# Queries in a four-block ring, and re-layout reads for one block at a time

## The chip, the cores and the metric

The kernel runs on one core of one Trainium2 chip. The metric is the device time of the whole program in microseconds (us), median of several runs. Before the change it is 1012.76 us (three runs: 1012.76, 1017.84, 1010.63).

## The reference

A pre-norm transformer layer in float32 on 2048 tokens of width 640: attention with 32 heads of 20, a causal sliding window of 256 keys, then a gated feed-forward of width 1536.

```
h  = x + softmax(mask(q k^T / sqrt(20))) v @ wo     with q,k,v = layernorm(x) @ wqkv
h2 = h + (gelu(layernorm(h) @ w_gate) * (layernorm(h) @ w_up)) @ w_down
mask: 0 <= i - j < 256
```

The kernel keeps float32 accuracy with float16 operands by splitting each operand into a high and a low half and adding three products.

## The kernel before

**Tiles.** The 2048 tokens are 16 blocks of 128 (index j) and 8 chunks of two blocks (index c). Queries and keys are projected a chunk at a time (`qk`, dense work on TensorE), values a block at a time (`vproj`). Scores and maxima work on a block and a pair of heads: 16 pairs for each block, and each block looks at three key blocks, its own and the two before it.

**Queries and keys on the way.** The projection leaves features on partitions in an order that the scores cannot use. So `qk_out` splits the result into halves (tile `qks`) and writes them to a DRAM tensor `qk` (a DMA issued by ACT), and `stack` reads that back in the layout that the scores need: tile `qT` for queries, the ring `kT` of six blocks (RK = 6) for keys. Each `stack` issues six DMAs, each of 20 partitions by 16 head pairs, on SP. There are two stacks for a chunk, so 12 reads of 160 KB for each chunk. The queries of a chunk have one tile `qT` from a pool with two buffers, so chunk c goes into the buffer that chunk c - 2 used. Before that the two buffers hold the raw query weights.

**Maxima, scores, values.** `maxima` multiplies queries (60 rows) by keys into the PSUM buffer `ra` or `rb`, and DVE takes the row maximum (`junk<-ra,band`, result in `mxs`). When all 32 heads of a block have one, the maximum is turned and written into rows 60 and 61 of `qT` (`qT<-mT`, a DMA issued by ACT), and `scores` computes the keys-by-queries product with the maximum already taken off (62 rows), ACT takes the exponential (`pt`), POOL masks it, and `value_lane` multiplies by the values into `pv`. The TensorE groups of maxima and scores come in pairs, one in `ra` and one in `rb`; between the pairs stand values and dense work.

**What sets the order.** Nothing is ordered by hand. A planner (the loop at the end of `block_kernel`) runs a clock for every engine and issues the next instruction of that lane which its clock says is ready, so a change in when one tile is free re-orders all engines. Each engine then executes its own list strictly in order on the chip. A `stack` begins when the planner's conditions hold: for chunks 0 and 1 when the split query weights are ready, later when block 2c - 3 has all its values (`B[2 * c - 3].scored`), which frees `qT` and the two key slots. From chunk 2 on there is also a pacing condition (`PACE`) ahead of each read, so other transfers come between. SP issues the input rows (`xt<-in_x_dram`, which the layer norm on DVE reads: `lstx<-xt`), the transposes of the normed rows (`xh<-xp`, `xl<-xp`), the residual rows (`ht<-in_x_dram`), the weight slices (`wsl`) and these reads, all in one list.

**Feed-forward.** When no projection is left, the first part of the feed-forward fills TensorE (`first_feed_forward`), and after the last block the rest follows, with TensorE alone in charge of the pace.

In the profile every instruction has the line L199, since one helper records all operations, so tiles tell them apart.

## Time and profile before

| | before |
|---|---|
| runs | 1012.76 us, 1017.84 us, 1010.63 us |
| profiled execution | 1014.85 us, span 1013.1 us |
| PE busy | 984.8 us (97%) |
| DVE, ACT, POOL busy | 753.8, 442.5, 312.9 us |
| `qT<-qk` and `kT<-qk` reads | 48 and 48, 160 KB each |
| DMA | 105853 packets, 112.96 MB, mean 111 GB/s |
| mean granted TensorE clock | 0.995 |

TensorE (PE) is in the chain that ended last for 79% of the span. A busy PE here means that at least one matmul was under way; the idle time ahead of an instruction stands in square brackets in the timeline, with what released it. The attention lasts until about 575 us and the feed-forward from there to the end. Inside the attention PE is not always busy, and the stretches in which it waits are short and few, so they can be looked at one by one.

### The profile page before, as it was taken

What the parts mean: (1) busy time and instruction counts of PE and PEld (TensorE: products, weight loads), DVE (VectorE), ACT (ScalarE), POOL (GpSimd) and SP (SyncE); (2) the same over time, 40 slices, a digit from 0 to 9 for tenths busy, and PEclk for the clock granted to TensorE, in tenths of its full rate; (3) what the DMA queues carried; (4) which work ended last, traced back from release to release, by engine and by line L of the source; (5) the groups of instructions that cost most, each with busy time, mean ns of one, the idle gap of its engine ahead of it and who ended that gap; (6) DMA issues with size and microseconds to landing.
All of it is one profiled execution on the core that took longest, in us unless ns stands there. A gap on an engine that the chain in (4) does not pass through costs nothing.

```text
span 1013.1 us, 35002 instructions
## 1 busy us (share of the span) xinstructions
PE 984.8 (97%) x15048; PEld 717.2 (71%) x15048; DVE 753.8 (74%) x2212; ACT 442.5 (44%) x711; POOL 312.9 (31%) x504
## 2 busy tenths in 40 slices
PE   8999999999989999999899999999999999999998
PEld 7777777777767777776656654567777777777775
DVE  7878999786767777776688787798888875554553
ACT  5616566755545555555566734332222222221220
POOL 7004344543333333333335401254313300000000
PEclk9999999999999999999999999999999999999999
DMA  8659596271471613414303442323553542222111
GB/s 309 139 133 185 155 183 186 65 166 34 95 123 42 144 46 70 104 33 93 133 29 107 94 146 75 107 102 117 145 181 105 159 139 68 79 104 85 73 53 53
DMA packets 105853, 112.96 MB, mean 111 GB/s; under 512 B 38369, under 2 KB 79585, under 8 KB 105697
## 3 DMA queue, kind: packets, MB, share of 16 engines
q1 hardware_dynamic: 93600, 99.97, 36.4%
q10 hardware_dynamic: 12096, 10.75, 3.6%
q8 instruction: 118, 1.93, 0.8%
q14 instruction: 39, 0.31, 0.1%
HBM read 73.73 MB, written 28.84 MB: 101 GB/s over the span
## 4 chain that ended last, share of the span: by engine, by line
PE 79%; DVE 8%; DMA 7%; issue 2%; ACT 2%; SPq 1%; POOL 0%; ACTq 0%; DVEq 0%; POOLq 0%
PE mm L199 39%; PE pv L199 12%; PE ra L199 12%; PE rb L199 9%; PE tp L199 7%; DVE junk L199 3%; DMA xt<-in_x_dram 1%; SPq L199 1%; DMA qT<-qk 1%; DMA qk<-qks 1%; DMA xl<-xp 1%; DVE am L199 1%; ACT pt L199 1%; DMA kT<-qk 1%; DMA qT<-mT 1%
## 5 line engine op out<-in xcount | busy, mean ns | idle before, releaser
L199 POOL TENSOR_SCALAR_AFFINE_SELECT pt<-pt 128x512 f32<-128x512 f32 x352 | 174.7, 512 | 288.8 <-ACT pt L199 276.0
L199 DVE CUSTOM_DVE_ANT_0 junk<-ra,band 128x320 bf16<-128x320 f32 x230 | 112.4, 489 | 46.8 <-PE ra L199 41.9
L199 ACT ACTIVATE pt<-rb,esc 128x640 f32<-128x640 f32 (+2 forms) x133 | 100.1, 761 | 78.1 <-PE rb L199 68.1
L199 DVE CUSTOM_DVE_ANT_0 junk<-rb,band 128x320 bf16<-128x320 f32 x218 | 106.5, 489 | 34.2 <-PE rb L199 28.9
L199 ACT ACTIVATE pt<-ra,esc 128x640 f32<-128x640 f32 (+2 forms) x123 | 94.5, 773 | 83.1 <-PE ra L199 68.6
L199 PE MATMUL pv<-pt,v 128*21 128x128 f32 x2880 | 104.6, 277 | 1.0 <-issue 0.8
L199 PEld LDWEIGHTS <-ah 128*128 128x128 f16 (+1 forms) x780 | 75.2, 98 | 28.6 <-issue 1.6
L199 ACT ACTIVATE gel<-gel,ffk 128x512 f32<-128x512 f32 x36 | 26.0, 722 | 140.6 <-DVE gel L199 136.1
L199 PEld LDWEIGHTS pv<-pt,v 128*21 128x21 f32 x2880 | 69.5, 101 | 11.6 <-issue 1.9
L199 PEld LDWEIGHTS <-kT 62*64 62x64 f16 x2880 | 64.6, 107 | 16.8 <-issue 13.0
L199 PEld LDWEIGHTS <-ws 128*128 128x128 f16 x720 | 70.5, 98 | 8.1
L199 PEld LDWEIGHTS <-qT 60*64 60x64 f16 x1280 | 30.0, 104 | 64.7 <-issue 54.5
L199 PEld LDWEIGHTS <-gu 128*128 128x128 f16 (+1 forms) x629 | 44.6, 98 | 32.9
L199 DVE SCALAR_TENSOR_TENSOR ht<-mm,ffk,ht 128x320 f32<-128x320 f32 x96 | 52.2, 545 | 14.4 <-PE mm L199 12.5
L199 ACT CAST ah<-gel 128x512 f16<-128x512 f32 x48 | 29.7, 618 | 71.0 <-DVE gel L199 70.8
L199 PE MATMUL mm<-xh,w1h 128*32 128x256 f16 (+1 forms) x383 | 56.3, 274 | 1.5 <-ACT qks L199 1.5
L199 PE MATMUL mm<-xl,w1h 128*32 128x256 f16 (+1 forms) x374 | 56.4, 274 | 0.2 <-issue 0.2
L199 PE MATMUL mm<-xh,w1l 128*32 128x256 f16 (+1 forms) x386 | 56.3, 273 | 0.0
L199 PE MATMUL mm<-xl,w0h 128*32 128x256 f16 (+1 forms) x358 | 49.1, 273 | 1.1 <-DMA xl<-xp 1.1
L199 PE MATMUL mm<-w3h,oh 128*32 128x320 f16 (+1 forms) x343 | 49.6, 300 | 0.4 <-DVE qks L199 0.4
L199 POOL TENSOR_TENSOR gelt<-gelt 128x256 f32<-128x256 f32 x18 | 15.6, 867 | 109.9 <-ACT gelt L199 109.9
L199 PE MATMUL mm<-w3l,oh 128*32 128x320 f16 (+1 forms) x346 | 49.5, 299 | 0.0
(313 smaller groups left out, 2592.7 us busy)
## 6 DMA issues: line engine op xcount, KB each, us to landing
ws<-wsums SPq DMA_DIRECT2D x24, 640.0 KB
qk<-qks ACTq DMA_DIRECT2D x32, 256.0 KB
qT<-qk SPq DMA_DIRECT2D x48, 160.0 KB
kT<-qk SPq DMA_DIRECT2D x48, 160.0 KB
wsums<-ws SPq DMA_DIRECT2D x12, 640.0 KB
ht<-in_x_dram SPq DMA_DIRECT2D x16, 320.0 KB
h_dram<-ht SPq DMA_DIRECT2D x16, 320.0 KB
ht<-h_dram SPq DMA_DIRECT2D x16, 320.0 KB
```

Source lines behind the costliest of these rows:

```text
L199: r = real(*args, **kw)
```

## The change

The queries go into one tile `qT` that is a ring of four blocks (RQ = 4), as the keys already had a ring of six. It takes the same room in SBUF as the two buffers did. Block j has slot j mod 4. From the third chunk on (c of 2 or more) `stack` is queued once for each block instead of once for the chunk: each reads one block's 128 columns, so there are 24 reads of 80 KB for a chunk in place of 12 of 160 KB, with pieces of 256 bytes in place of 512. Each block's reads have a condition of their own: block b may begin when block b - 4 has all its values. For the second block of a chunk that is the old condition, for the first block it is one block earlier. A block's maxima may begin when its own queries and keys are there. Chunks 0 and 1 are read as before, in one piece.

```diff
-    RV, RK = 5, 6
+    RV, RK, RQ = 5, 6, 4
     kT = wp.tile([P, H // 2, RK, P], F16, name="kT")
+    qT = wp.tile([P, H // 2, RQ, P], F16, name="qT")
...
-            side.append((LATE, stack(c, which, d)))
-
-    def stack(c, which, d):
+            for blocks in [[2 * c, 2 * c + 1]] if c < 2 else [[2 * c], [2 * c + 1]]:
+                side.append((LATE, stack(c, which, d, blocks)))
+
+    def stack(c, which, d, blocks):
+        last = blocks[-1]
         yield ("sync",), need(d, when=lambda: pos["big"] == 2 and (W["q"].ready if c < 2 else
-                                                                B[2 * c - 3].scored), eng="sync")
+                                                                B[last - 4].scored), eng="sync")
...
-            to = C[c].qT
-        else:
-            s = 2 * c % RK
-            to = kT[:, :, s:s + 2, :].rearrange("p i r n -> p i (r n)")
+        ring, n = ((qT, RQ), (kT, RK))[which]
+        s = blocks[0] % n
+        to = ring[:, :, s:s + len(blocks), :].rearrange("p i r n -> p i (r n)")
+        cols = slice(blocks[0] % 2 * P, blocks[-1] % 2 * P + P)
...
                 nc.sync.dma_start(to[rows], d.rearrange("(a d i) m n -> a m d i n", a=2,
-                                                        d=DH)[par, i])
-        C[c].stacked += 1
-        if C[c].stacked == 2:
-            for b in (2 * c, 2 * c + 1):
+                                                        d=DH)[par, i][:, :, cols])
+        for b in blocks:
+            B[b].stacked += 1
+            if B[b].stacked == 2:
                 for pr in range(0, H // 2, pairs(b)):
                     heapq.heappush(maxq, (b, pr))
```

The users of `qT` (`maxima`, `row_need`, `max_transpose`, `scores`) take slot j mod 4 in place of the chunk's tile.

Because the planner re-orders everything, the lists of the engines differ in most places. Three places matter below.

SP's list where the third chunk (blocks 4 and 5) is read, before: 12 reads, with `qk` numbers 1656 for queries and 2141 for keys.

```order
L199 DMA qT<-qk_1656 20x16x256 x2
L199 DMA h_dram<-ht 128x640
L199 DMA qT<-qk_1656 20x16x256 x4
L199 DMA kT<-qk_2141 20x16x256
L199 DMA_TRANSPOSE xh<-xp 128x5x128
L199 DMA kT<-qk_2141 20x16x256
L199 DMA_TRANSPOSE xl<-xp 128x5x128
L199 DMA xt<-in_x_dram 128x640
L199 DMA kT<-qk_2141 20x16x256 x3
L199 DMA wsl<-in_wg_dram 128x512
L199 DMA kT<-qk_2141 20x16x256
```

The same place now (queries 1682, keys 2287): the reads of block 5's queries stand ahead of block 4's keys, which are the first six of the `kT` reads.

```order
L199 DMA qT<-qk_1682 20x16x128 x6
L199 DMA xt<-in_x_dram 128x640
L199 DMA h_dram<-ht 128x640
L199 DMA wsl<-in_wg_dram 128x512
L199 DMA qT<-qk_1682 20x16x128 x5
L199 DMA wsl<-in_wg_dram 128x512
L199 DMA qT<-qk_1682 20x16x128
L199 DMA kT<-qk_2287 20x16x128 x2
L199 DMA_TRANSPOSE xh<-xp 128x5x128
L199 DMA_TRANSPOSE xl<-xp 128x5x128
L199 DMA xt<-in_x_dram 128x640
L199 DMA kT<-qk_2287 20x16x128 x2
```

Here twice as many reads are in SP's list, at the same place in the program, and two loads of input rows stand behind or between them.

SP's list where the fifth chunk (blocks 8 and 9) is read, before: queries 3714, keys 4547, and the transposes and input rows of two later blocks between them.

```order
L199 DMA qT<-qk_3714 20x16x256 x4
L199 DMA_TRANSPOSE xh<-xp 128x5x128
L199 DMA_TRANSPOSE xl<-xp 128x5x128
L199 DMA xt<-in_x_dram 128x640
L199 DMA qT<-qk_3714 20x16x256 x2
L199 DMA kT<-qk_4547 20x16x256 x3
L199 DMA_TRANSPOSE xh<-xp 128x5x128
L199 DMA_TRANSPOSE xl<-xp 128x5x128
L199 DMA xt<-in_x_dram 128x640
L199 DMA kT<-qk_4547 20x16x256 x3
```

The same chunk now (queries 4204, keys 4678): block 8 is read first, then come residual rows, two transposes with input rows, and then block 9.

```order
L199 DMA qT<-qk_4204 20x16x128 x6
L199 DMA kT<-qk_4678 20x16x128 x6
L199 DMA ht<-in_x_dram 128x640
L199 DMA_TRANSPOSE xh<-xp 128x5x128
L199 DMA_TRANSPOSE xl<-xp 128x5x128
L199 DMA xt<-in_x_dram 128x640
L199 DMA h_dram<-ht 128x640
L199 DMA ht<-in_x_dram 128x640
L199 DMA_TRANSPOSE xh<-xp 128x5x128
L199 DMA_TRANSPOSE xl<-xp 128x5x128
L199 DMA xt<-in_x_dram 128x640
L199 DMA qT<-qk_4204 20x16x128 x6
```

The input rows that stood among the reads of one chunk now stand between the two groups of its reads, with the transposes.

PE's list late in the attention, where the last block's value projection is not yet free to run, before: the values of a unit (`pv`) are followed at once by the next maxima (`ra<-kT,qT`), with no dense matmul between.

```order
L199 MATMUL pv<-pt,v_122 21x128 x4
L199 MATMUL pv<-pt,v_121 21x128 x4
L199 MATMUL pv<-pt,v_123 21x128 x4
L199 LDWEIGHTS qT
L199 MATMUL ra<-kT,qT 64x320
```

Now, at the corresponding place, the value projection of blocks 14 and 15 (`mm<-w2h,xl` and its likes) follows the values.

```order
L199 MATMUL pv<-pt,v_122 21x128 x4
L199 MATMUL pv<-pt,v_121 21x128 x4
L199 MATMUL pv<-pt,v_123 21x128 x4
L199 LDWEIGHTS xl
L199 MATMUL mm<-w2h,xl 32x320
L199 LDWEIGHTS xl
L199 MATMUL mm<-w2h,xl 32x320
```

Before, four units in a row had no dense matmul between their pairs there; now each unit at this place has some.

## The prediction

> **What bounds the kernel now.** First the page's busy times and the windows by stage, to see which engine sets the pace where. Columns of the windows: length, busy time of PE, weight loads, DVE, ACT, POOL, then granted clock, DMA share, GB/s.

> ```profile
> span 1013.1 us, 35002 instructions
> PE 984.8 (97%) x15048; PEld 717.2 (71%) x15048; DVE 753.8 (74%) x2212; ACT 442.5 (44%) x711; POOL 312.9 (31%) x504
> 140.00:280.00 140.00, 134.96 (x3110) 103.69 (x3108) 112.41 (x410) 86.53 (x139) 64.39 (x117) 0.99 0.47 119
> 280.00:420.00 140.00, 135.68 (x3336) 103.27 (x3335) 100.34 (x366) 73.83 (x115) 51.30 (x107) 0.99 0.42 87
> 420.00:560.00 140.00, 135.03 (x3176) 94.15 (x3163) 103.33 (x357) 84.28 (x128) 59.34 (x115) 0.99 0.28 81
> 560.00:1013.10 453.10, 445.06 (x3419) 309.48 (x3416) 319.42 (x659) 124.26 (x193) 94.27 (x97) 1.00 0.33 105
> ```

> PE is busy 97% and nothing else above 74%. So PE's list sets the time, and a gain can come from two places only: less work in that list, or less waiting in it. In the three windows of the attention PE misses 5.0, 4.3 and 5.0 us, some 14 us. The feed-forward after 560 us uses no query and no key.

> Next the places where PE waits, from PE's timeline (start, length, what, and in brackets the idle time ahead with its releaser).

> ```profile
> 225.89 0.32 PE L199 MATMUL ra<-kT,qT 60*64 60x256 f16 x5
> 229.12 0.32 PE L199 MATMUL ra<-kT,qT 60*64 60x64 f16 x3 [2.91 <-DMA kT<-qk]
> 289.49 0.34 PE L199 MATMUL ra<-qT,kT 62*64 62x128 f16 x12 [3.13 <-DVE mxs L199]
> 470.82 0.33 PE L199 MATMUL rb<-qT,kT 62*64 62x128 f16 x11 [1.08 <-issue]
> 482.15 0.33 PE L199 MATMUL ra<-kT,qT 60*64 60x320 f16 x4 [0.68 <-ACT pt L199]
> 482.80 0.34 PE L199 MATMUL rb<-qT,kT 62*64 62x128 f16 x12 [0.32 <-DVE mxs L199]
> 485.42 0.48 PE L199 MATMUL rb<-kT,qT 60*64 60x320 f16 x4 [0.90 <-ACT pt L199]
> ```

> The first is the start of block 6: its keys, read with chunk 3, have not landed. The second names DVE, so DVE's and SP's lists come next.

> ```profile
> 287.62 0.89 DVE L199 BATCH_NORM_STATS2 lstx<-xt 128x6 f32<-128x320 f32 x2 [3.56 <-DMA xt<-in_x_dram]
> 276.41 0.57 SPq L199 DMA_DIRECT2D xt<-in_x_dram  x1
> 277.04 1.58 SPq L199 DMA_DIRECT2D qT<-qk  x2
> 278.67 2.31 SPq L199 DMA_DIRECT2D kT<-qk  x3
> 281.12 2.78 SPq L199 DMA_TRANSPOSE xh<-xp  x1
> ```

> DVE stood still for 3.56 us for input rows issued at 276.41 and landed near 287.6, 11.2 us later: they were in the queue with the reads of chunk 4 and two transposes. DVE works strictly in order, so the maxima behind this instruction waited, and PE behind them. So the two longest waits of the attention come from the reads of a whole chunk (chunks 3 and 4).

> After such waits the clock falls. Windows of 5 us:

> ```profile
> 225.00:230.00 5.00, 2.09 (x52) 1.44 (x45) 1.84 (x5) 1.10 (x4) 1.42 (x3) 0.91 0.64 124
> 230.00:235.00 5.00, 5.00 (x89) 3.19 (x90) 2.06 (x10) 1.77 (x3) 1.93 (x4) 0.75 0.02 5
> 290.00:295.00 5.00, 4.96 (x92) 3.50 (x90) 3.38 (x17) 1.91 (x3) 1.70 (x4) 0.66 0.82 185
> 485.00:490.00 5.00, 4.35 (x78) 2.88 (x78) 3.31 (x13) 2.75 (x5) 2.20 (x5) 0.66 0.96 295
> ```

> Each place loses 1.7 us more: 5 x (0.09 + 0.25) and 5 x 0.34. So a wait of 2.9 us costs 4.6 us.

> **The change part by part.** *PE's work.* The same maxima, scores, values and projections are computed, in another order. What an order can change is how often PE passes between 64-row groups, 32-column groups and full matmuls, and how many dense matmuls are cut into four.

> ```profile
> 247.00 0.29 PE L199 MATMUL mm<-xl,w0h 128*32 128x256 f16 x4
> 247.11 0.29 PE L199 MATMUL mm<-xh,w0l 128*32 128x256 f16 x4
> 249.43 0.27 PE L199 MATMUL mm<-xh,w0l 128*128 128x256 f16 x1
> 249.54 0.27 PE L199 MATMUL mm<-xh,w0h 128*128 128x256 f16 x1
> 249.74 0.33 PE L199 MATMUL rb<-kT,qT 60*64 60x256 f16 x8
> ...
> 235.18 0.85 PE L199 MATMUL pv<-pt,v 128*21 128x128 f32 x24
> 235.84 0.32 PE L199 MATMUL mm<-w2l,xh 128*32 128x320 f16 x4
> 235.98 0.32 PE L199 MATMUL mm<-w2h,xl 128*32 128x320 f16 x4
> ...
> 247.66 0.33 PE L199 MATMUL ra<-kT,qT 60*64 60x256 f16 x8
> 247.82 0.31 PE L199 MATMUL rb<-qT,kT 62*64 62x128 f16 x12
> ```

> Four quarters take 0.11 us from start to start (247.00 to 247.11), one whole matmul 0.11 (249.43 to 249.54): the cut costs nothing, and that the new list has fewer of them (w0h high by high: 49 sets in place of 59) gives nothing. A passage costs 0.1 us (249.54 to 249.74 is 0.20). Counted in the two lists from the first maxima to the last values there are 525 passages before and 526 now: 0.1 us. The new list has 15 more filler matmuls (`pv<-ident`) in the start-up, where PE waits for data anyway: 0, at most 0.8 us at 0.056 each, which is an estimate from half a 256-column row. So PE's work is the same, and everything hangs on waits.

> *The reads.* For a chunk 12 reads of 160 KB become 24 of 80 KB. Their price, from chunk 7, where little else moves:

> ```profile
> 456.16 4.72 SPq L199 DMA_DIRECT2D qT<-qk  x6
> 460.92 7.93 SPq L199 DMA_DIRECT2D kT<-qk  x6
> 456.16:473.00 16.84, 15.71 (x400) 11.37 (x401) 9.75 (x37) 9.17 (x16) 5.66 (x12) 1.00 0.67 139
> ```

> SP issues the first six in 0.79 us each; the next take 1.32 each, because the queue is full. A half read has the same 320 pieces. Its time in the queue lies between 0.66 us (half the bytes) and 1.32 us (the same pieces); SP's issue alone asks 0.79. I take 0.9, nearer to the low end, since 0.79 bounds it from below: 24 x 0.9 is 22 us for a chunk where there were 16, and 11 us for a block's 12. [...] No row here shows a 256-byte read from DRAM.

> *What the reads hide behind.* I measured the lead in the two lists: PE's work from the last read of keys to the first maxima that use them, priced by the rows above (0.11 and 0.14 us for a dense matmul of 256 and 320 columns, 0.16 for a group of maxima or scores, 0.67 for a unit of values, 0.1 for a passage). Before, chunks 2 to 7 have 9.3, 4.2, 4.4, 5.5, 8.4 and 5.6 us; the wait at 226 is where it is 4.2. Now block 4 has 7.7, block 14 has 17, block 12 has 25, and the nine others 35 to 42. The lead counts from the last read, so 17 us cover it even with a whole block's reads queued ahead at the high price (12 x 1.32 is 16). So from block 5 on no maxima wait for keys: the wait at 226 goes with its clock, 2.9 + 1.7 = 4.6 us. If that cover were gone, it would come back.

> *The input rows.* In SP's list chunk 4's rows now stand between the reads of blocks 8 and 9, not inside them. I let the wait at 286 go: 3.1 + 1.7 = 4.8 us.

> *The thin place.* At 481 to 486 four pairs follow each other with values but no dense matmul (three of the rows above), so PE waits for ACT and DVE: 0.68 + 0.32 + 0.90, and the clock 1.7, 3.6 us. In the new list the value projection of blocks 14 and 15 fills this place. I let the 3.6 go; bounds 0 and 3.6, since nothing else of the order is known to cost there.

> *What is new: chunk 2.* Its 24 reads stand where 12 stood, and there the queue is busiest.

> ```profile
> 100.00:125.00 25.00, 24.72 (x530) 18.71 (x522) 23.83 (x81) 15.21 (x27) 8.33 (x11) 1.00 0.61 166
> 125.00:150.00 25.00, 23.60 (x494) 18.00 (x488) 23.57 (x87) 15.08 (x25) 10.29 (x18) 1.00 0.90 179
> 150.00:175.00 25.00, 24.68 (x579) 19.57 (x570) 24.09 (x85) 16.62 (x28) 11.72 (x20) 1.00 0.69 191
> ```

> At 0.90 there is room for 2.5 us in the middle window. The new reads bring 6 us (0.9 each) to 16 (1.32 each), at the share 0.67 of the row above 4 to 11 us of all engines. They spread over some 35 us, so they fit badly, and two loads of input rows stand among them; DVE, busy 23.6 of 25 us there, cannot catch up. Block 4's keys come behind block 5's queries with a lead of 7.7 us in place of 9.3. I count one wait of the size of that at 286, 4.8 us; bounds 0 and 9.4 (that and the one at 226).

> *The rest.* Of the short waits that I let stand from 60 us on, these are the first and the last of eight; the eight sum to 6.4 us.

> ```profile
> 93.38 0.27 PE L199 MATMUL mm<-xl,w0h 128*128 128x256 f16 x1 [1.07 <-DMA xl<-xp]
> ...
> 550.70 0.52 PE L199 MATMUL ra<-qT,kT 62*64 62x128 f16 x10 [0.69 <-DMA qT<-mT]
> ```

> A new list has short waits of its own in their stead that nobody can read off. I add 2, bounds -4 and +6.

> **Sum.** Against the profiled execution of 1014.85 us (span 1013.1): -4.6 - 4.8 - 3.6 + 4.8 + 2 = -6.2, so 1008.6. That execution lies 2.1 above the median 1012.76, so on the scale of the median it is **1006.5 us**.

> **The rivals.** *All waits go.* If half reads are as cheap as their issue, chunk 2 adds nothing and the new list is lucky by 2: -13.0 - 2 = -15.0, 998 us. For it: leads of 17 to 42 us. Against: chunk 2's lead shrank. Chance 0.26.

> *The gain is eaten.* A half read costs as much as a whole one, 1.32 us: 9.4 us of waits at chunk 2 and 5 of new ones: -13.0 + 14.4 = +1.4, 1014 us. For it: 512-byte pieces run at 139 GB/s in the row above while whole-row loads reach 295 at 485. [...] Chance 0.16.

> *Slower.* Input rows late at every load. In the new SP list four loads of input rows come right behind reads (three at chunk 2, one at chunk 4); a late one halts DVE and, by the row at 287.62, costs PE 4.8 us. All four and the keys of block 4: 4 x 4.8 + 4.6 = 23.8, less 13.0, is +10.8, 1024 us. It decides from the third late load on, where the gain is used up. Against: before, four loads stood so (one at chunk 2, one at chunk 3, two at chunk 4), and one wait came of it. Chance 0.10.

> My forecast, a loss of waits that leaves -2 to -10, has 0.48: 1002 to 1011.

> **Numbers.** The range 997 to 1017 leaves out half of the lucky case and most of the slow one. For this kernel a measurement tells about 1% (10 us) from no change: faster by over 1% means under 1002.6, which takes the 0.26 and a little of the forecast's edge, 0.29; slower means over 1022.9, the 0.10; within 1% the rest, 0.61.

> **What would show it.** Right: no wait of PE on `kT<-qk` after 175 us and none near 227; DVE's longest wait for `xt<-in_x_dram` at 115 to 160 us or gone; SP's reads of a block in 9 to 12 us; dense matmuls between the pairs of the last three blocks; PE's busy time unchanged to within 3 us. Wrong: six half reads on a full queue at 1.3 us each; PE misses more than 5 us in 100 to 180; new waits on ACT's DMAs (`qk<-qks`, `qT<-mT`); or a busy PE that is longer, which would mean that the order costs work after all.

## The result, and the profile after

The changed kernel takes 1002.86 us (median; 1001.09, 1002.69, 1003.03, 1004.52), the kernel before 1012.71 us in the same runs. The ratio is 0.9895, with a 95% interval of 0.9855 to 0.9935. The forecast was 1006.5 us, the range 997 to 1017. The profiled execution is the one of 1001.09 us.

The page of the changed kernel, and the windows by stage of both kernels (the first four rows before, the last four after; columns as in the prediction):

```profile
span 999.4 us, 34564 instructions
PE 982.2 (98%) x14781; PEld 715.2 (72%) x14781; DVE 747.9 (75%) x2212; ACT 441.8 (44%) x711; POOL 313.7 (31%) x504
```

```profile
60.00:100.00 40.00, 38.89 (x715) 29.20 (x716) 33.19 (x142) 18.71 (x40) 9.78 (x13) 1.00 0.82 172
100.00:175.00 75.00, 73.00 (x1583) 56.27 (x1571) 71.49 (x251) 46.92 (x78) 30.34 (x48) 1.00 0.73 178
175.00:575.00 400.00, 387.23 (x9232) 285.62 (x9225) 294.71 (x1046) 231.47 (x360) 165.71 (x327) 0.99 0.36 86
575.00:1013.10 438.10, 430.24 (x3056) 299.17 (x3056) 307.44 (x630) 113.46 (x175) 85.80 (x80) 1.00 0.32 105
```

```profile
60.00:100.00 40.00, 37.61 (x528) 25.81 (x527) 34.88 (x148) 16.18 (x37) 7.87 (x11) 0.95 0.73 158
100.00:175.00 75.00, 72.14 (x1452) 54.88 (x1450) 67.02 (x244) 45.99 (x76) 33.50 (x50) 0.98 0.67 173
175.00:575.00 400.00, 398.75 (x9353) 297.18 (x9352) 301.30 (x1067) 241.25 (x376) 166.97 (x330) 1.00 0.36 92
575.00:999.40 424.40, 418.16 (x2966) 290.07 (x2963) 300.10 (x620) 106.93 (x165) 84.03 (x78) 1.00 0.33 106
```

What PE misses in a row is its length less its busy time. From 175 to 575 us it was 12.8 us and is 1.3; the half-clock stretches shown in the prediction (225 to 235, 290 and 485 us, 5.1 us together) are gone too. That is 16.6 us. From 60 to 175 us PE missed 3.1 us and misses 5.3, and here there is new half clock (0.50 from 97 to 103 us):

```profile
95.00:100.00 5.00, 3.23 (x25) 1.98 (x26) 4.40 (x16) 3.37 (x6) 0.86 (x1) 0.64 0.65 204
100.00:105.00 5.00, 5.00 (x63) 3.31 (x61) 3.79 (x15) 4.62 (x8) 2.67 (x4) 0.68 0.82 211
```

5 x (0.36 + 0.32) is 3.4 us, so the early part gives back 5.5 us. After 575 us 1.6 us less is missed. The sum is -12.7 of the 13.7 us between the two spans. The profiled execution of before was 2.1 us above its median and this one 1.8 us below its own, so some 4 of the 13.7 us are the scatter of executions.

These are PE's waits of over 0.6 us between 40 and 600 us after the change, from its timeline:

```profile
54.14 0.30 PE L199 MATMUL ra<-kT,qT 60*64 60x128 f16 x7 [0.62 <-DMA kT<-qk]
96.64 0.48 PE L199 MATMUL ra<-kT,qT 60*64 60x320 f16 x4 [1.66 <-DVE mxs L199]
153.69 0.34 PE L199 MATMUL ra<-qT,kT 62*64 62x128 f16 x12 [0.63 <-ACT pt L199]
162.02 0.33 PE L199 MATMUL ra<-kT,qT 60*64 60x320 f16 x4 [1.83 <-ACT pt L199]
```

Between 162 and 484 us no wait is longer than 0.3 us, and after the first row no maxima wait for keys. The wait at 286 us went as well: DVE's longest wait for input rows is 1.4 us, in the start-up at 3.9 us, where 3.56 stood. Not every wait of PE is followed by half clock: after the 1.83 us at 162 us the granted clock is 1.00 from 160 to 170 us.

```profile
DVE lstx L199 <- DMA xt<-in_x_dram: 1.4, 1, 1.4
```

The half reads, from SP's timeline, with the row of SP's transfer queue from the page (packets, MB, share of 16 engines' span), before and then after:

```profile
372.34 4.73 SPq L199 DMA_DIRECT2D kT<-qk  x6
383.88 5.10 SPq L199 DMA_DIRECT2D qT<-qk  x6
```

```profile
q1 hardware_dynamic: 93600, 99.97, 36.4%
```

```profile
q1 hardware_dynamic: 117360, 99.97, 36.5%
```

Six half reads take 4.7 to 5.1 us, SP's issue rate. The queue's time is 0.364 x 16 x 1013.1 = 5900 us before and 0.365 x 16 x 999.4 = 5836 after, for the same bytes in 23760 more packets.

**The wait at 162 us.** It names ACT. Followed back, first SP's waits for that releaser between 149 and 160 us (total, times, longest), then the timelines of SP and ACT:

```profile
SPq L199 <- DMA qk<-qks: 3.0, 1, 3.0
```

```profile
150.62 2.31 SPq L199 DMA_DIRECT2D kT<-qk  x3
155.97 0.74 SPq L199 DMA_DIRECT2D kT<-qk  x1
156.82 0.45 SPq L199 DMA_DIRECT2D wsl<-in_wg_dram  x1
153.31 0.37 ACTq L199 DMA_DIRECT2D qk<-qks  x1
153.77 0.75 ACTq L199 DMA_DIRECT2D qk<-qks  x1
159.75 0.72 ACT L199 ACTIVATE gu<-wsl,sw 128x512 f16<-128x512 f32 x1 [2.29 <-DMA wsl<-in_wg_dram]
```

A read of chunk 2's keys stood 3.0 us for a write of products that ACT issued at 153 us. By count (six such writes a chunk) that write holds chunk 3's queries, while chunk 2's products had all been written by 138 us. Behind the read stood a weight slice; ACT waited 2.29 us for it, and PE behind ACT. Why a read of one chunk waits for the products of another was the question of the experiments.

### The profile page after: what moved, and what is told of

The parts are those of the page before. It is cut to its first block, busy times and chain, and to the rows that moved or that the text cites. A ratio compares the mean times of both kernels' runs of the same rounds, so it can differ in the third digit from the quotient of the medians.

```text
span 999.4 us, 34564 instructions
## 1 busy us (share of the span) xinstructions
PE 982.2 (98%) x14781; PEld 715.2 (72%) x14781; DVE 747.9 (75%) x2212; ACT 441.8 (44%) x711; POOL 313.7 (31%) x504
## 4 chain that ended last, share of the span: by engine, by line
PE 78%; DVE 5%; ACT 2%; DMA 1%; issue 1%; SPq 0%; POOL 0%; ACTq 0%; DVEq 0%; POOLq 0%
PE mm L199 37%; PE pv L199 12%; PE ra L199 12%; PE rb L199 10%; PE tp L199 7%; DVE am L199 1%; DVE ts L199 1%; DMA wst<-in_wu_dram 0%; DVE gel L199 0%; DVE ws L199 0%; ACT pt L199 0%; DVE junk L199 0%; DVE ht L199 0%; DMA xt<-in_x_dram 0%; DVE al L199 0%
## 5 line engine op out<-in xcount | busy, mean ns | idle before, releaser
L199 POOL TENSOR_SCALAR_AFFINE_SELECT pt<-pt 128x512 f32<-128x512 f32 x352 | 174.6, 511 | 271.0 <-ACT pt L199 253.2
L199 DVE CUSTOM_DVE_ANT_0 junk<-ra,band 128x320 bf16<-128x320 f32 x230 | 112.5, 489 | 40.5 <-PE ra L199 35.7
L199 ACT ACTIVATE pt<-rb,esc 128x640 f32<-128x640 f32 (+2 forms) x131 | 99.7, 768 | 92.4 <-PE rb L199 73.9
L199 DVE CUSTOM_DVE_ANT_0 junk<-rb,band 128x320 bf16<-128x320 f32 x218 | 106.7, 489 | 34.1 <-PE rb L199 29.0
L199 ACT ACTIVATE pt<-ra,esc 128x640 f32<-128x640 f32 (+2 forms) x125 | 95.0, 767 | 71.1 <-PE ra L199 60.7
L199 PE MATMUL pv<-pt,v 128*21 128x128 f32 x2880 | 103.1, 276 | 0.8 <-ACT oT L199 0.6
L199 PEld LDWEIGHTS <-ah 128*128 128x128 f16 x768 | 75.1, 98 | 28.4 <-issue 1.2
L199 ACT ACTIVATE gel<-gel,ffk 128x512 f32<-128x512 f32 x36 | 26.0, 722 | 136.8 <-DVE gel L199 136.8
L199 PEld LDWEIGHTS <-ws 128*128 128x128 f16 x720 | 70.4, 98 | 9.2 <-DVE ws L199 1.1
L199 PEld LDWEIGHTS pv<-pt,v 128*21 128x21 f32 x2880 | 69.1, 100 | 10.4 <-issue 1.5
L199 PEld LDWEIGHTS <-qT 60*64 60x64 f16 x1280 | 30.0, 104 | 63.4 <-issue 52.4
L199 PEld LDWEIGHTS <-kT 62*64 62x64 f16 x2880 | 64.6, 107 | 10.0 <-issue 6.4
L199 PEld LDWEIGHTS <-gu 128*128 128x128 f16 (+1 forms) x629 | 44.1, 98 | 33.4
L199 DVE SCALAR_TENSOR_TENSOR ht<-mm,ffk,ht 128x320 f32<-128x320 f32 x96 | 52.1, 545 | 15.4 <-PE mm L199 13.4
L199 ACT CAST ah<-gel 128x512 f16<-128x512 f32 x48 | 29.6, 617 | 72.4 <-DVE gel L199 70.8
L199 PE MATMUL mm<-xh,w1h 128*32 128x256 f16 (+1 forms) x356 | 55.9, 273 | 0.9 <-DVE qks L199 0.9
L199 PE MATMUL mm<-xh,w1l 128*32 128x256 f16 (+1 forms) x362 | 56.0, 273 | 0.0
L199 PE MATMUL mm<-xl,w1h 128*32 128x256 f16 (+1 forms) x368 | 55.9, 273 | 0.0
L199 POOL TENSOR_TENSOR gelt<-gelt 128x256 f32<-128x256 f32 x18 | 15.7, 872 | 111.0 <-ACT gelt L199 110.9
L199 PE MATMUL mm<-xl,w0h 128*32 128x256 f16 (+1 forms) x325 | 49.5, 275 | 0.0
L199 PE MATMUL mm<-xh,w0h 128*32 128x256 f16 (+1 forms) x322 | 49.5, 275 | 0.0
L199 PE MATMUL mm<-w3h,ol 128*32 128x320 f16 (+1 forms) x322 | 49.4, 299 | 0.0
```

What stands on the lines that cost most here:

```text
L199: r = real(*args, **kw)
```

## The experiments

The theory at the start was that of the prediction: what gains is the lead, above all because the first block of a chunk may be read one block earlier, and half reads are cheap. The rivals: the ring alone does it; the halves do it without the earlier start; any other order of the planner moves the time as much. The comparison of SP's waits then brought a second theory, that SP's reads stand behind unrelated writes of ACT because the two share completion counters.

| kernel | median us | ratio to before, 95% interval |
|---|---|---|
| the change | 1002.86 | 0.9895 (0.9855 to 0.9935) |
| e1_ring_only | 1007.15 | 0.9951 (0.9928 to 0.9973) |
| e2_old_start | 1026.0 | 1.0128 (1.0098 to 1.0158) |
| e4_reads_twice | 1063.53 | 1.0507 (1.0476 to 1.0537) |
| e8_all_blocks | 1014.2 | 1.0012 (0.9992 to 1.0032) |
| e10_from_chunk3 | 1001.4 | 0.99 (0.9864 to 0.9935) |
| e5_before_lead21 | 1006.49 | 0.9955 (0.9931 to 0.998) |
| e6_before_apart | 1011.53 | 1.0007 (0.9979 to 1.0034) |
| e7_after_lead21 | 1003.83 | 0.9913 (0.9882 to 0.9943) |
| e11_after_apart | 1004.35 | 0.9917 (0.9884 to 0.9951) |
| e14_from_chunk3_lead21 | 999.63 | 0.9867 (0.9836 to 0.9899) |
| e15_old_start_pool | 1001.68 | 0.9891 (0.9856 to 0.9925) |
| e16_after_pool | 999.09 | 0.9863 (0.9833 to 0.9894) |

### The ring alone

```diff
-            for blocks in [[2 * c, 2 * c + 1]] if c < 2 else [[2 * c], [2 * c + 1]]:
+            for blocks in [[2 * c, 2 * c + 1]]:
```

For a whole chunk the condition `B[last - 4].scored` is the old one, since its last block is 2c + 1.

> Queries in the ring of four, but the reads as before: whole reads for both blocks of a chunk, started when the chunk's old condition holds. The times to compare with are 1012.7 us (before) and 1002.9 us (after). If the gain is in the leads (a block's keys landing before its row pairs), it is not here: the 12 whole reads still take 1.32 us each and start no earlier, a wait of PE for keys comes back between 200 and 310 us, and the time is 1009 to 1014. If the ring by itself gives it (queries of two chunks no longer share their tiles): 1001 to 1005, with no wait for keys. If it is only that the planner rolled another order: anywhere from 1000 to 1018, with waits at new places.

1007.15 us, between the first two cases and inside the third, wide one. PE's timeline has a wait for keys again; late in the attention it has two waits that name no engine ("issue"), with dense matmuls between the pairs:

```profile
289.09 0.33 PE L199 MATMUL ra<-kT,qT 60*64 60x320 f16 x3 [1.63 <-DMA kT<-qk]
459.29 0.28 PE L199 MATMUL rb<-qT,kT 62*64 62x128 f16 x7 [1.39 <-issue]
484.56 0.32 PE L199 MATMUL mm<-w2h,xh 128*32 128x320 f16 x4
486.94 0.60 PE L199 MATMUL tp<-ident,o 128*128 128x128 f32 x4 [1.25 <-issue]
```

So the thin place of 481 to 486 us is filled here too, and from 200 to 530 us PE has no wait of over 0.1 us for ACT or DVE. But from 175 to 575 us it misses 8.6 us, where the changed kernel misses 1.3: the ring alone leaves a part of the gain out. Of the 8.6 us, 5.4 are five waits that name no engine. Each of them ends 1.4 to 1.6 us after a 16 KB packet of the instruction queue (q8 on the page) has ended in the trace. That PE waits there for its own code is the author's reading of this; no run tests it. That this kernel is 5 us faster than before may be no more than its other order (see the section on orders).

### Halves on the old condition

```diff
-                                                                B[last - 4].scored), eng="sync")
+                                                                B[2 * c - 3].scored), eng="sync")
```

> The changed kernel with both blocks' reads held back to the old condition of the chunk; reads for one block at a time, of half the size, in the ring of four. Every engine but SP and ACT's few DMAs keeps the order of the changed kernel. If halves suffice (12 half reads of 0.79 us land the first block's keys 9.5 us after the start, where 12 whole ones took 15.8 us): 1002 to 1005, no wait for keys. If the early start is what counts: the 24 reads of a chunk lie together again and the loads of xt behind them are late, a wait of DVE for xt of about 3 us and one of PE of 3 us with 1.7 us at half clock at one chunk or two: 1006 to 1011.

1026.0 us: far above both cases. PE, DVE, ACT and POOL have the list of the changed kernel, so nothing but the places of SP's reads differs. PE's waits for keys summed (total, times, longest), and then from the timelines the first of them and chunk 3's 12 key reads:

```profile
PE ra L199 <- DMA kT<-qk: 16.1, 5, 6.0
```

```profile
233.05 0.32 PE L199 MATMUL ra<-kT,qT 60*64 60x64 f16 x3 [5.98 <-DMA kT<-qk]
216.59 18.89 SPq L199 DMA_DIRECT2D kT<-qk  x12
```

The 12 took 18.89 us, 1.57 each, twice the price of the rows at 372. They were not slow in the queue, they were issued late. SP's waits for products from 190 to 240 us, and from the timelines its reads in finer pieces and ACT's writes:

```profile
SPq L199 <- DMA qk<-qks: 11.6, 3, 5.1
```

```profile
222.46 2.31 SPq L199 DMA_DIRECT2D kT<-qk  x3
229.20 2.35 SPq L199 DMA_DIRECT2D kT<-qk  x3
220.31 0.37 ACTq L199 DMA_DIRECT2D qk<-qks  x1
227.06 0.37 ACTq L199 DMA_DIRECT2D qk<-qks  x1
```

Twice SP goes on 2.1 us after a write was issued. Those writes are chunk 4's keys. SP's list of this kernel, with the semaphores that each entry waits for (the first five of chunk 3's key reads; `DMAHW` with a number is the completion counter of a transfer):

```
L199 DMA kT<-qk_3349 20x16x128 [waits DMAHW6_49]
L199 DMA kT<-qk_3349 20x16x128 [waits DMAHW7_49]
L199 DMA kT<-qk_3349 20x16x128 [waits DMAHW0_49]
L199 DMA kT<-qk_3349 20x16x128 [waits DMAHW1_49]
L199 DMA kT<-qk_3349 20x16x128 [waits DMAHW2_49]
```

and ACT's first two writes of chunk 4's keys:

```
L199 DMA qk_4666<-qks 128x2x512 [waits DMAHW7_49,DVE_49]
L199 DMA qk_4666<-qks 128x2x512 [waits DVE_49]
```

The numbers run from 0 to 7. So there are eight counters, handed out in turn to the transfers of SP and of ACT, and each transfer waits until the one that had its counter before it has landed. The first read went out at 216.59. The second needs counter 7, as did ACT's write that left at 220.31, and it left at 222.46, 0.02 us after that write's last completion in the trace (222.44). The fifth needs counter 2 and left at 229.20, after the next write (issued at 227.06, completed at 229.19). So no more than eight transfers of both engines are under way (in the traces of before and after, too, eight at most), and if one of the last eight is a write whose product isn't computed yet, SP stands, with all that is behind it. 24 reads in one go take the eight round three times.

### The writes on other counters

```diff
-        nc.scalar.dma_start(d[ts[0] * P:(ts[-1] + 1) * P].rearrange("(t p) m n -> p t (m n)", p=P),
-                            both)
+        to = d[ts[0] * P:(ts[-1] + 1) * P].rearrange("(t p) m n -> p t (m n)", p=P)
+        nc.gpsimd.real.dma_start(to, both)
+        nc.issue("scalar", nc.scalar.cost("dma_start", to, [both]), [both], [to], 0.4)
```

The last line keeps the planner's clocks as they were. POOL's transfers have counters of their own (`DMASW0` to `DMASW7` in the lists of these kernels).

> The kernel with both blocks' reads on the old condition (1026.0 us), with the 48 writes of products to DRAM issued by POOL in place of ACT, at the same places of the program; PE, DVE and SP keep their order. The writes then no longer take one of the eight completion counters that SP's and ACT's transfers use in turn. If SP's reads in that kernel stood behind unrelated writes because each waits for the transfer that had its counter before (11.6 us of such waits between 190 and 240 us): the waits for keys at 227, 296 and 361 us (16.1 us together) shrink below 6 us and the time falls to 1005 to 1015, unless POOL, which now waits for the products, holds up the masks. If the late start and the number of reads are what made them late: the waits for keys stay near 16 us and the time at 1022 to 1030.

1001.68 us, 24 us less than the same kernel with ACT's writes. Chunk 3's key reads in SP's timeline, and PE's waits for keys summed:

```profile
212.15 9.46 SPq L199 DMA_DIRECT2D kT<-qk  x12
```

```profile
PE ra L199 <- DMA kT<-qk: 2.5, 3, 1.7
```

12 half reads take 9.46 us, 0.79 each, SP's issue rate. The waits for keys fell from 16.1 us to 2.5, and the mean granted clock of the profiled execution rose from 0.988 to 1.0. The edit also takes the issue of the writes off ACT, but in the kernel with ACT's writes PE's waits of over 0.5 us from 170 to 575 us all name keys, and none names ACT. So most of what the earlier start is worth is time to sit out SP's standing; what it is worth with free counters follows from the next run. POOL paid 0.73 us (median) for each of the 48 writes (its busy time went from 313.7 to 346.3 us), and PE's longest waits don't name it.

> The changed kernel with the 48 writes of products issued by POOL in place of ACT, the order of PE, DVE and SP kept. If the counters matter there too: the weight slice that was issued at 156.8 us, behind a read that stood 3.0 us for such a write, comes earlier, the wait of 1.83 us at 160 us goes, and the time is 999 to 1002. If POOL's masks come late behind its waits for products: waits of PE for POOL's pt, 1004 to 1015.

The same edit on the changed kernel: 999.09 us. As expected, the wait at 162 us is gone; from 152 to 170 us PE's only wait in the timeline is the one of 0.65 us at 153. It is clearly faster than before. Its interval (0.9833 to 0.9894) overlaps with that of the change (0.9855 to 0.9935), so that it beats the change too is likely, not certain. Against the old start with the same counters (1001.68) the earlier start still gains 2.6 us: the slowest of its executions (1000.17) is below the fastest of the other (1000.76), and PE has no wait for keys of over 0.3 us after 40 us where the other has 2.5 us. With ACT's writes the earlier start gained 23 us (1026.0 to 1002.86).

### Every half read twice

```diff
+        scr = dram.tile([6, DH, H // 2, P], F16, name=f"scr{blocks[0]}{which}") if c > 1 else None
...
                 nc.sync.dma_start(to[rows], d.rearrange("(a d i) m n -> a m d i n", a=2,
                                                         d=DH)[par, i][:, :, cols])
+                if c > 1:
+                    nc.sync.real.dma_start(scr[3 * par + m], d.rearrange(
+                        "(a d i) m n -> a m d i n", a=2, d=DH)[par, i][:, :, cols])
```

> The changed kernel, each half read followed on SP by a second read of the same pieces into a scratch in DRAM that nobody reads, in the same order on every engine. Two issues of 0.79 us make a half read cost 1.6 us of SP's queue, more than a whole read before (1.32 us). If the cheap half read is what the gain stands on: chunk 2's 24 reads take 38 us in place of 19 us, the loads of xt and of the weight slices wait behind them, PE loses 5 to 10 us there, and the time is 1008 to 1013. If the early start carries it (later chunks have 20 to 40 us of lead) and only chunk 2 is short: 1004 to 1008, with all new waits before 200 us. If the price of a read does not matter: 1002 to 1004.

1063.53 us, beyond all cases, and not for the price. The longest of PE's waits, the wait of ACT that it names, and SP's list ahead of it:

```profile
397.04 0.48 PE L199 MATMUL ra<-qT,kT 62*64 62x128 f16 x12 [27.83 <-ACT pt L199]
395.57 0.72 ACT L199 CAST xp<-xt 128x640 f16<-128x640 f32 x1 [29.57 <-DMA xl<-xp]
354.06 0.76 SPq L199 DMA_DIRECT2D kT<-qk  x1
368.48 0.51 SPq L803 DMA_DIRECT2D scr<-qk  x1
```

SP stood from 354.8 to 368.5 us, for a write of products that ACT issued at 365.74. Among its waits in the attention those for `qk<-qks` and `qT<-mT` are the largest. More reads followed, and the transpose `xl<-xp`, behind them in SP's list, left only at 392.9 us; ACT's next write of `xp` stood 29.57 us for it, and PE 27.83 us for ACT's exponentials. Twice as many reads take the same eight counters in turn, so this run adds to the standing (13.7 us in this one place) along with the price. It doesn't tell the price; the 9.46 us above do.

### Which chunks

Chunk 2 as before, single blocks from chunk 3 on:

```diff
-            for blocks in [[2 * c, 2 * c + 1]] if c < 2 else [[2 * c], [2 * c + 1]]:
+            for blocks in [[2 * c, 2 * c + 1]] if c < 3 else [[2 * c], [2 * c + 1]]:
```

> The changed kernel with chunk 2 read as before (12 whole reads for both blocks, the old condition) and single blocks only from chunk 3 on; every other engine keeps the order of the changed kernel. If the 24 reads at chunk 2 are a burden, as the forecast's +4.8 us had it: SP spends 16 us on them in place of 19 us, the weight slice behind them lands earlier, the wait of 1.83 us at 160 us goes, and the time is 1000 to 1002. If halves help there too (chunk 2's first block has its keys after 9.5 us in place of 15.8 us): a wait for keys of 2 to 6 us comes between 130 and 180 us and the time is 1005 to 1012.

1001.4 us, with PE's list unchanged. The weight slice is issued at 150.4 us in place of 156.8, and no wait above 0.3 us follows the one at 153 until 482. Of its span PE is idle 15.6 us in place of 17.2. Chunk 2's 24 reads were a burden, of some 1.6 us by the traces; the two times alone, with their wide intervals, don't tell it.

The same with the other bound on the maxima's lead:

> Single blocks from chunk 3 on, chunk 2 read as before, with the planner's bound on the maxima's lead at 21 (the changed kernel with that bound: 1003.8 us, with a wait of 3.12 us at 163 us). If chunk 2's 24 reads cost more than they bring, in this order too: that wait goes and the time is 998 to 1002. If the 1.5 us between chunk 2 whole and halved was nothing but the order: 1002 to 1008.

999.63 us against 1003.83 with single blocks from chunk 2 on: the wait of 3.12 us at 163 us is gone. Here PE's list differs as well, so the 4 us are not the reads' alone, but in neither order did halves at chunk 2 bring anything.

Chunk 1 by single blocks too (`if c < 1`):

> The changed kernel with chunk 1 also read one block at a time (from the second chunk on). If the leads give the gain, only the wait of 0.62 us for keys at 54 us can go, and the 24 reads fall in the stretch where the DMA share is highest: 1001 to 1005. If a new order by itself moves the time by as much as the change did: outside 998 to 1008.

1014.2 us: the whole gain is lost. Two rows of PE's timeline, the window with half clock, and SP's waits for products from 100 to 575 us:

```profile
86.27 0.31 PE L199 MATMUL rb<-qT,kT 62*64 62x128 f16 x8 [2.88 <-DVE mxs L199]
163.47 0.33 PE L199 MATMUL rb<-kT,qT 60*64 60x320 f16 x3 [2.86 <-DMA kT<-qk]
```

```profile
100.00:105.00 5.00, 4.93 (x45) 2.73 (x49) 4.59 (x19) 2.99 (x5) 0.63 (x2) 0.50 0.86 261
```

```profile
SPq L199 <- DMA qk<-qks: 99.8, 19, 23.1
```

SP stands 99.8 us for writes of products (69.0 in the changed kernel), and keys are late again. But its order differs everywhere, so how much of the 11 us belongs to the reads stays open.

### Other orders of the same reads

Before and after with one number of the planner changed, so that the same instructions come in another order:

```diff
-    LEAD, TARGET = 20, 0.0
+    LEAD, TARGET = 21, 0.0
```

```diff
-    AHEAD, APART = 0.2, 1.0
+    AHEAD, APART = 0.2, 0.9
```

> The kernel before, with the planner's bound on how far the maxima run ahead of the second pass at 21 in place of 20: the same work and the same reads, another order. If what a new order does by itself is small beside the change: 1008 to 1017, within 0.5% of before. If the order alone moves the time as much as the change did: outside 1003 to 1022, with waits at other places than 226 and 286 us.

> The kernel before, with the planner's distance between row pairs at 0.9 us in place of 1.0 us: the same work and the same reads, another order. If what a new order does by itself is small: 1008 to 1017. If the order alone moves the time as much as the change did: outside 1003 to 1022.

> The changed kernel with the planner's bound on the maxima's lead at 21 in place of 20: another order with the early single-block reads. If the reads give the gain and not this one order: 1000 to 1007, with no wait for keys after 175 us. If the gain is this order's: 1008 to 1018.

> The changed kernel with the planner's distance between row pairs at 0.9 us in place of 1.0 us (before with that order: 1011.5 us). If early single-block reads give the gain and the order only scatters it: 1000 to 1007. If the gain is one order's luck: 1008 to 1016.

| planner | before, us | after, us | ratio after less ratio before | PE misses from 175 to 575 us, before and after, us |
|---|---|---|---|---|
| as it is | 1012.71 | 1002.86 | -0.0105 | 12.8 and 1.3 |
| LEAD 21 | 1006.49 | 1003.83 | -0.0042 | 8.5 and 2.0 |
| APART 0.9 | 1011.53 | 1004.35 | -0.0090 | 5.7 and 2.0 |

An order by itself moves the kernel before by 6 us, more than half of the gain, and the expected 1008 to 1017 was too narrow at LEAD 21. The changed kernel stays within 1.5 us in all three. After is faster in each pair by the medians (at LEAD 21 the two intervals overlap), by 8 us on average (mean of the ratios' differences, 0.0079, of 1012.7). So the change helps, and the 9.85 us contain some luck of the old order.

The last column says this more plainly than the times: after 175 us the changed kernel leaves PE almost no wait in any of the three orders. It gives some back earlier: from 60 to 175 us PE misses 3.1, 3.3 and 6.2 us before, and 5.3, 6.1 and 7.1 after. The two waits that the prediction set out from, however, belong to one order. In the other two orders of the kernel before DVE has no wait of over 0.3 us for input rows after the start-up, and PE's longest waits for keys are 0.75 and 0.59 us.

A part of what goes with the whole reads is PE's waits that name no engine. Between 100 and 575 us the four kernels that read whole chunks (before in its three orders, and the ring alone) have ten of over 0.6 us. The ten kernels with half reads have one, of 1.62 us at 156 us, in the kernel at LEAD 21 that reads chunk 2 whole just before. All eleven end 1.3 to 1.7 us after an instruction packet has ended. Some of them stand where SP issues no read, as the one at 487 us with the ring alone: that the whole reads are the cause is not shown.

## Why the prediction was right

**The keys at 226 us (-4.6): right in size, the cause not complete.** The wait and its half clock are gone. The prediction put the late keys down to the queue's price and a lead of 4.2 us. In the kernel before, SP's waits between 205 and 220 us and its timeline show also this:

```profile
SPq L199 <- DMA qk<-qks: 4.0, 1, 4.0
```

```profile
209.61 0.74 SPq L199 DMA_DIRECT2D kT<-qk  x1
214.47 1.62 SPq L199 DMA_TRANSPOSE xh<-xp  x1
218.42 5.85 SPq L199 DMA_DIRECT2D kT<-qk  x5
```

Five of the six key reads stood behind a transpose that waited 4.0 us for a write of products, of chunk 4 by count. Unlike the writes in the run with halves on the old condition, this one was not issued late. ACT issued it at 207.33 us, and by the trace its last completion came 7.1 us later, at 214.40; the six query reads issued from 203.40 to 207.38 us completed 4.9 to 7.9 us after their issue, each taking longer than the one before it. So the queue was behind, as the prediction had it, and the shared counter passed this on to the transpose and to all that stood behind it. Without those 4 us the 2.91 us wait would have been covered, if nothing else had come in between; the kernel before with POOL's writes was not tried.

**The input rows at 286 us (-4.8): right.** Gone, with DVE's wait for them. It is gone with the ring alone as well, and in the two other orders of the kernel before, so another order is enough for that. That DVE's maxima stood behind the rows, as the prediction had it, shows in the trace of before: PE had filled `ra` by 284.52 us, and DVE read it at 288.43, right after the statistics of those rows.

**The thin place (-3.6): right.** One wait of 0.39 us is left there (at 484 us), and it names no engine. The ring alone fills the place too, and the kernel before at APART 0.9 has no wait of over 0.3 us from 407 to 545 us, while at LEAD 21 it waits 1.54, 0.56 and 0.96 us between 462 and 477 us. So it is the order that fills the place, and single blocks are not needed for it.

**Chunk 2 (+4.8): the step that failed.** The early part did give back 5.5 us, but not as argued; that this is near 4.8 is luck. No load of input rows was late. The DMA share from 125 to 150 us did not rise from 0.90. It fell:

```profile
125.00:150.00 25.00, 25.00 (x521) 20.09 (x520) 23.43 (x88) 14.86 (x26) 9.40 (x18) 1.00 0.54 147
```

Chunk 2's own cost is some 1.6 us (the run that leaves it whole), through a counter, a weight slice and ACT. The prediction had named new waits on ACT's writes as a sign against it, and did not price them. The other 3.4 us and more are the half clock after the wait at 96 us, which stands ahead of chunk 2's first read (118 us) and stays when chunk 2 is read whole: it comes with the new order and not with the reads.

**The rest (+2): wrong in sign.** In 400 us, from 175 to 575, PE misses 1.3 us in all: of the eight short waits, the six that stood there (3.9 us) were not replaced by others, and two of these six, 0.84 us at 298 and 1.08 at 471, name no engine and end 1.52 and 1.44 us after an instruction packet has ended. With that and the 1.6 us after 575 us the profiled gain was 13.7 and not 6.2.

**A half read (0.9 us, bounds 0.66 and 1.32).** Its price is SP's issue, 0.79 to 0.85 us in a burst of six (372 and 384 us) and 0.79 in one of twelve, so the rival in which the gain is eaten falls. The queue keeps up: in the burst of twelve each read completed 3.0 to 4.6 us after its issue, where the whole reads at 203 us took 4.9 to 7.9 and those of chunk 7, at which the prediction called the queue full, 4.5 to 8.4. With the reads from chunk 2 on in pieces of 256 bytes in place of 512 the queue's time is 5836 us against 5900. At 36% of its time the queue is far from full on average, so what pieces of either size cost on a full queue is not shown.

**PE's work.** 982.2 us for 984.8. The 2.6 us are near the 1.7 us less of half clock (5.1 before, 3.4 after), so the order itself cost no work.

The time, 1002.86, lies between the forecast's 1006.5 and the rival in which all waits go (998). A ratio of 0.9895 with its interval is at the border between "faster by over 1%" and "within 1%", where the prediction had put 0.29 and 0.61. The rival on the slow side had its point of decision at three late loads of input rows, and there was none. The mean gain over three orders, 0.79%, is nearer to the forecast of 6.2 us than the one order that was timed.

## What to carry to other kernels

When a transfer comes late, look first at when it was issued and what its queue stood for, and only then at its price: here a run of small reads waited for writes that had nothing to do with it, and other counters for the writes cured it, or an earlier start that left time to sit it out. More and smaller transfers use up such a shared resource faster even where their bytes cost the same (24 half reads take the eight counters three times round, 12 whole ones one and a half), so split only those that have lead to spare. And where a planner re-orders everything, time the change in two or three orders before the last half per cent is believed.

## What the runs showed of the hardware

The fourth is behind the costliest wait that is left, 1.66 us at 96 us with half clock after it. DVE's and POOL's timelines of the changed kernel just ahead of it, and then the row of that DVE operation over the whole run (duration in ns, least, median, most):

```profile
93.77 1.22 DVE L199 TENSOR_TENSOR lyx<-lyx,lyax 128x1 f32<-128x1 f32 x1
93.57 1.40 POOL L199 TENSOR_TENSOR w3l<-wsl,w3h 128x640 f16<-128x640 f32 x1
```

```profile
L199 DVE TENSOR_TENSOR lyx<-lyx,lyax x13: 149/159/1220, 7.0 to 338.1; 128x1 f32<-128x1 f32 x13
```

A product of one element per partition, 0.16 us as a rule, took 1.22 us and ended (94.99) when POOL's subtraction ended (94.97). The same holds in the kernel before at 107 us, where 0.92 us end at 108.44 and POOL's subtraction at 108.42. That DVE is held for what is left of POOL's operation is the author's reading of these times; by what, the traces do not show. Not every operation of DVE is longer beside one of POOL: in the changed kernel `gel<-ra,rs`, with one input in PSUM, takes 405 to 417 ns in all 36 cases, seven of them beside an instruction of POOL. `al<-gel,ah`, with both inputs in SBUF, takes 628 to 693 ns in 35 of its 48 cases, one of them beside POOL's, and 797 to 1636 ns in the other 13, all beside POOL's for 0.25 us or more. The 1.06 us lost here stand in DVE's list ahead of the maxima for which PE waited 1.66 us, and half clock after it cost 3.4 us more. Whether the wait goes when POOL's operation is moved was not tried.
